# The fourth pair's bit rows: from SyncE's DMA queue to GpSimd's own queue

## The chip, the cores and the metric

The kernel runs on one core of one Trainium2 chip. The metric is device time in microseconds (us), lower is better; times are medians of several executions. TensorE (PE) multiplies matrices, VectorE (DVE), ScalarE (ACT) and GpSimd (POOL) work elementwise, and SyncE (SP) issues nearly all DMAs. Each engine carries out its own instructions in order and waits for others through semaphores; a DMA is issued by an instruction in one engine's order and lands later.

## The reference

Hash attention, then a gated feed-forward block with a residual. For 4 batches, 8 heads, 768 positions and 64 dimensions per head, a query sees only the keys that fall into its own hash bucket; the bucket is given by the signs of 6 projections.

```python
q_bits = (np.einsum('bhsd,dk->bhsk', q, proj) > 0)
k_bits = (np.einsum('bhsd,dk->bhsk', k, proj) > 0)
mask = q_bucket[:, :, :, None] == k_bucket[:, :, None, :]
scores = np.where(mask, scale * (q @ k.T), -1e9)
attn = softmax(scores)                      # over the keys
x = (attn @ v)                              # heads side by side: 3072 x 512
g, val = x @ w_gate, x @ w_val              # 512 -> 1536
ffn = (gelu(g) * val) @ w_out               # 1536 -> 512
out = x + sigmoid(x @ w_res) * ffn
```

## The kernel before

The 32 heads are worked on as 16 pairs, numbered 0 to 15; the fourth pair is number 3, the sixth number 5. Four pairs make a batch. For a pair, q and k (tiles `ld`) and v (`ldv`) are loaded. q and k are cast to bf16 (`cast`, tile `nat`) and transposed, mostly by a DMA transpose on SP (`transpose_dma`, into `aug`). `aug` holds the first head's 64 transposed dimensions; those of the second head are copied by GpSimd into the lower half of a tile `second` (`move_second`, L214).

The mask is put into the matmul itself. VectorE transposes blocks of q and k (`blocks`, L245, tile `t`), TensorE multiplies them with the projections (`hash_half`, L282), VectorE makes the signs (`hb`, L288) and shuffles them into the right partitions (`spread`, L297, tile `bits`). Then `mask_rows` (L322 to L329) moves seven rows of signs for each head and side into `aug` or `second` by four small DMAs, 10.5 KB each, two to `second` and then two to `aug`. With these rows the score matmul gives a large bonus to keys of the same bucket, and the exponential does the rest. So scores of a pair (L441, tile `sp`) can't start before its rows have landed.

A pair's scores are made in 9 chunks (12 for pair 0). For a chunk TensorE makes scores into one of two `sp` banks, ScalarE takes the exponential (L445, `e`), and two chunks later TensorE multiplies it with the values (L412) into the one `av` bank. At the pair's end VectorE normalises (`rec` L388, `x_tok` L389), which frees that bank, and TensorE transposes the outcome into `x_sb`. At a batch's end gate and value matmuls (`gate_val`, L463) follow, four chunks into the next batch, and the projection (`project`, L483 and L498) is spread over the chunks of the next batch.

The order is written by hand: `at(slot, f, ...)` puts work into a chunk's slot, and each engine gets its instructions in the order in which slots and tasks are walked through. `b1`, `b2` and `b3` are the first slots of pairs 1, 2 and 3. Within a slot the order of the `at` calls decides. No planner changes it on this path. Pools decide what has to wait: three `ld` buffers per side, two of `ldv`, `nat` and `bits`, four of `aug`. SP takes its DMAs one after the other; one of them waiting for a buffer or an earlier DMA holds the rest.

Around the change, in pair 1's last slots, SP issues loads of pair 3's v and of q and k of pairs 6 and 7, then pair 3's rows, then pair 4's v, its transposes and the first weight loads (`load_w`, L179). GpSimd has `move_second` of pair 3, the casts of pair 5, then `values_prep` of pair 3 (v to bf16 and sums over v, L332 to L340), then `move_second` of pair 4. Pair 1's rows are already divided between the two queues: `at(7, mask_rows, 1, (nc.sync, nc.gpsimd))`.

Of the kernel before, what the change touches and what calls it, by code (L numbers as in the profile page):

```python
# [17 lines left out]
def kernel(  # L18
# [12 lines left out]
    nc = tc.nc  # L31
# [485 lines left out]
    def base(p):  # L517
        return order.index((p, 0))
# [10 lines left out]
    def at(slot, f, *args):  # L529
        if f in (hash_half, transpose_pe):  # L530
            uses_tp.add(slot)
        tasks[slot].append(lambda: f(*args))
        busy[slot] += cost.get(f, 0.0)
# [88 lines left out]
    b1, b2, b3 = (base(i) for i in (1, 2, 3))  # L622
# [25 lines left out]
        at(b1 + 7, spread, 3, a)  # L648
    for side in range(2):
        at(b1 + 6, move_second, (3, side))  # L650
        at(b1 + 7, cast, (5, side))
        at(b1 + 7 + side, blocks, (5, side))
    at(b1 + 7, load, 7, (0, 1))
    at(b1 + 8, mask_rows, 3)
    at(b1 + 8, values_prep, 3)

    at(b2, load, 4, (2,))
# [139 lines left out]
```

## Time and profile before

| | |
|---|---|
| median of 6 runs | 348.25 us (347.44 to 349.45) |
| the profiled execution | 348.09 us, of which its span from the first to the last instruction 346.3 us |
| TensorE busy | 333.6 us, 96% of the span |
| ScalarE busy | 210.6 us, 61% |
| VectorE busy | 153.2 us, 44% |
| GpSimd busy | 153.2 us, 44% |
| DMA | 44.04 MB, mean 127 GB/s |
| exponentials, L445 | 147 of them, 143.7 us, mean 1007 ns |
| TensorE clock granted | 0.999 |

The share of busy time is a mean over stages. Up to about 53 us the first batch's attention runs without other work for TensorE beside it; afterwards feed-forward matmuls fill it. In a timeline each line has the start, the duration, the engine, the source line, the operation and its tiles; brackets hold the idle time before it and what ended it. SPq is SP's queue of DMA issues: the duration there is that of issuing, not of the transfer.

### The profile page before, as it was taken

The page shows a single profiled execution, that of the slowest core. Times are in us where ns is not written, and L with a number is a line of the kernel's source. Part 1 is how long each engine was busy: PE and PEld are TensorE (multiplying, and loading weights), DVE is VectorE, ACT ScalarE, POOL GpSimd, SP SyncE. Part 2 cuts the span into 40 slices and gives each one's busy share as a digit, 9 for nine tenths or more (in the row PEclk, how much of TensorE's full clock was granted, in tenths as well). Part 3 has the DMA queues.
Part 4 walks back from the last instruction along what each step waited for, and adds up shares of the span by engine and source line. Part 5 has one row for each costly group of instructions (what it writes and reads, how often), then busy time and mean ns, then how long its engine had stood idle before and what let it go on. Part 6 is the DMA issues. An engine that isn't in the chain of part 4 may idle for free.

```text
span 346.3 us, 7432 instructions
## 1 busy us (share of the span) xinstructions
PE 333.6 (96%) x2961; PEld 196.2 (57%) x3010; DVE 153.2 (44%) x280; ACT 210.6 (61%) x238; POOL 153.2 (44%) x198
## 2 busy tenths in 40 slices
PE   8889789999999999999999999999999999999995
PEld 4555556565565565655456566565556665665443
DVE  7986822333136526333444446343452026334243
ACT  6889885325898885223888788223788883332220
POOL 5899486864479585200068589300038222000000
PEclk9999999999999999999999999999999999999999
DMA  7977999997706964720014783600003321000012
GB/s 223 273 239 197 284 337 195 328 345 148 257 8 171 213 200 80 212 92 2 0 38 129 196 190 105 163 5 1 2 3 93 55 55 61 2 0 2 30 61 91
DMA packets 52717, 44.04 MB, mean 127 GB/s; under 512 B 31656, under 2 KB 44620, under 8 KB 52684
## 3 DMA queue, kind: packets, MB, share of 16 engines
q1 hardware_dynamic: 52540, 43.56, 45.3%
q8 instruction: 23, 0.38, 0.4%
q14 instruction: 10, 0.08, 0.1%
q0 software_dynamic: 64, 0.02, 0.0%
q10 hardware_dynamic: 80, 0.00, 0.0%
HBM read 29.36 MB, written 6.29 MB: 103 GB/s over the span
## 4 chain that ended last, share of the span: by engine, by line
PE 83%; ACT 4%; DVE 4%; POOL 3%; DMA 2%; issue 2%; SPq 1%; DVEq 0%; ACTq 0%; POOLq 0%
PE sp L463 36%; PE fps L498 16%; PE sp L441 13%; PE av L412 8%; PE rps L483 5%; ACT e L445 4%; PE hs L282 4%; DMA ld<-in_k_dram 2%; SPq L95 1%; DVE x_tok L389 1%; POOL ldv L338 1%; PE tp L398 1%; POOL o L507 1%; DVE o L504 1%; DVE total L382 1%
## 5 line engine op out<-in xcount | busy, mean ns | idle before, releaser
L445 ACT ACTIVATE e<-sp 128x1024 bf16<-128x1024 f32 (+1 forms) x147 | 143.7, 1007 | 25.4 <-PE sp L441 22.1
L469 ACT ACTIVATE gt<-sp 128x768 bf16<-128x768 f32 x48 | 38.9, 811 | 83.0 <-PE sp L463 83.0
L470 DVE SCALAR_TENSOR_TENSOR hh<-gt,sp 128x768 bf16<-128x768 bf16 x48 | 45.8, 954 | 81.4 <-PE sp L463 81.4
L498 PE MATMUL fps<-wo,hh 128*128 128x512 bf16 (+2 forms) x285 | 74.3, 369 | 1.3
L463 PE MATMUL sp<-x_sb,wg 128*128 128x256 bf16 (+1 forms) x376 | 70.3, 325 | 0.4
L463 PE MATMUL sp<-x_sb,wv 128*128 128x256 bf16 (+1 forms) x376 | 69.8, 325 | 0.6 <-DVE hh L470 0.2
L412 PEld LDWEIGHTS <-e 128*128 128x128 bf16 x1152 | 50.3, 97 | 33.5 <-issue 8.7
L441 PE MATMUL sp<-aug,aug 71*128 71x512 bf16 x192 | 54.3, 326 | 3.0 <-ACT e L445 2.9
L412 PE MATMUL av<-va,e 128*128 128x65 bf16 x1152 | 56.1, 193 | 1.0 <-DVE x_tok L389 0.3
L463 PEld LDWEIGHTS <-wv 128*128 128x128 bf16 x384 | 37.5, 98 | 25.2 <-issue 0.4
L463 PEld LDWEIGHTS <-wg 128*128 128x128 bf16 x384 | 37.2, 98 | 24.4
L441 PE MATMUL sp<-second,second 128*128 128x256 bf16 (+1 forms) x174 | 47.4, 320 | 0.3 <-ACT e L445 0.3
L507 POOL TENSOR_TENSOR o<-o,x_tok 128x512 f32<-128x512 f32 x18 | 20.8, 1156 | 56.7 <-DVE o L504 49.4
L498 PEld LDWEIGHTS <-hh 128*128 128x128 bf16 x300 | 28.6, 97 | 27.1
L504 DVE SCALAR_TENSOR_TENSOR o<-th,fps 128x512 f32<-128x512 f32 (+2 forms) x25 | 16.5, 661 | 52.7 <-PE fps L498 41.4
L389 POOL TENSOR_TENSOR x_tok<-total,rec 128x768 bf16<-128x768 f32 x9 | 13.3, 1472 | 45.0 <-DVE rec L388 45.0
L214 POOL COPY second<-aug 64x768 bf16<-64x768 bf16 x29 | 23.6, 825 | 19.6 <-DMA aug<-nat 12.9
L245 DVE STREAM_TRANSPOSE t<-ld 128x768 f32<-128x768 f32 (+1 forms) x34 | 29.5, 903 | 3.9 <-DMA ld<-in_q_dram 3.5
L486 ACT ACTIVATE th<-rps 128x512 f32<-128x512 f32 x24 | 14.3, 596 | 18.7 <-PE rps L483 14.3
L483 PE MATMUL rps<-wr,x_sb 128*128 128x512 bf16 x96 | 24.6, 379 | 0.0
L441 PEld LDWEIGHTS <-second 128*128 128x128 bf16 x192 | 18.5, 98 | 5.6 <-issue 2.5
L441 PEld LDWEIGHTS <-aug 71*128 71x128 bf16 x192 | 16.2, 97 | 6.7 <-issue 1.7
(71 smaller groups left out, 231.0 us busy)
## 6 DMA issues: line engine op xcount, KB each, us to landing
ldv<-in_v_dram SPq DMA_DIRECT2D x16, 384.0 KB
out_dram<-o SPq DMA_DIRECT2D x23, 256.0 KB
ld<-in_q_dram SPq DMA_DIRECT2D x15, 384.0 KB
ld<-in_k_dram SPq DMA_DIRECT2D x15, 384.0 KB
ws<-in_moe_w_gate_dram SPq DMA_DIRECT2D x6, 512.0 KB
ws<-in_moe_w_val_dram SPq DMA_DIRECT2D x6, 512.0 KB
ws<-in_moe_w_out_dram SPq DMA_DIRECT2D x6, 512.0 KB
ws<-in_moe_w_res_dram SPq DMA_DIRECT2D x2, 512.0 KB
```

What stands on the lines that cost most here:

```text
L214: eng.tensor_copy(second[x[0] % NM][x[1]][D:P], aug[x][D:P])
L245: nc.vector.transpose(t32[x][:, c0:c1].rearrange("p c h n -> p (c h n)"), raw[x][:, c0:c1].rearrange("p c d -> p (c d)"))
L412: nc.tensor.matmul(o[:, qt0 + i, :], e[:, off + i * P:off + (i + 1) * P], va[:, hi, jt, 0:D + 1], start=(hi not in begun), stop=(jt == T - ...
L441: nc.tensor.matmul(sp[:, off:off + nq * P], ks[0:n, jt, :], qs[0:n, qt0:qt0 + nq, :], start=True, stop=True)
L445: nc.scalar.activation(e[:, 0:n], sp[:, 0:n], AF.Exp, scale=float(ALPHA))
L463: nc.tensor.matmul(sp[:, c0:c1], w[:, kk, bass.ts(m, P)], xs[:, kk, c0:c1], start=(kk == 0), stop=(kk == KM - 1))
L469: nc.scalar.activation(gt, sp[:, 0:S], AF.Gelu)
L470: nc.vector.scalar_tensor_tensor(hh[:, m, :], gt, 0.5, ps[1][:, 0:S], op0=ALU.mult, op1=ALU.mult)
L483: nc.tensor.matmul(rps, x_sb[b][:, kk, t, :], wr[:, kk, :], start=(kk == 0), stop=(kk == KM - 1))
L498: nc.tensor.matmul(fps, hh[:, m, bass.ts(t, P)], wo[:, m, cs], start=(m == 0), stop=(m == KF - 1))
L504: nc.vector.scalar_tensor_tensor(o[:, cs], th[:, cs], 1.0, fps, op0=ALU.add, op1=ALU.mult)
L507: last.tensor_add(o3, o3, x_tok[b][:, k0:k1, t, :])
```

## The change

`mask_rows` of pair 3 goes from slot `b1 + 8` to slot `b1 + 7`, and its four DMAs are issued by GpSimd instead of SP. The two casts of pair 5 go from slot `b1 + 7` to `b1 + 8`, so that on GpSimd they follow these DMAs. On SP the four are gone from between the loads of pair 7 and the load of pair 4's v; the order of everything else on every engine is unchanged.

```diff
     for side in range(2):
         at(b1 + 6, move_second, (3, side))
-        at(b1 + 7, cast, (5, side))
         at(b1 + 7 + side, blocks, (5, side))
+
+    at(b1 + 7, mask_rows, 3, (nc.gpsimd, nc.gpsimd))
+    for side in range(2):
+        at(b1 + 8, cast, (5, side))
     at(b1 + 7, load, 7, (0, 1))
-    at(b1 + 8, mask_rows, 3)
     at(b1 + 8, values_prep, 3)
```

## The prediction

> **What bounds the kernel now.** I read the page first (TensorE busy 96% of a span of 346.3 us), then the list of waits, then the timelines of each queue and engine around the rows that move. The rows are those of pair 3, the fourth. Their wait stands in the list of waits between 24 and 60 us:
>
> ```profile
> PEld L441 <- DMA aug<-bits: 1.2, 1, 1.2
> ```
>
> It happens once. The timelines of the weight loads, of TensorE and of ScalarE place it (columns: start, duration, engine, line, operation, tiles; in brackets the idle time before and its releaser):
>
> ```profile
> 39.46 0.10 PEld L441 LDWEIGHTS <-aug 71*128 71x128 bf16 x1 [1.24 <-DMA aug<-bits]
> 39.49 0.38 PE L441 MATMUL sp<-aug,aug 71*128 71x512 bf16 x1 [1.15 <-ACT e L445]
> ...
> 35.41 3.87 ACT L445 ACTIVATE e<-sp 128x1024 bf16<-128x1024 f32 x4 [0.23 <-PE sp L441]
> 40.18 4.69 ACT L445 ACTIVATE e<-sp 128x1024 bf16<-128x1024 f32 x5 [0.90 <-PE sp L441]
> ```
>
> The first scores of pair 3 (L441) stand still until the rows land at about 39.4; the releaser beside the matmul is only inferred, the weight load in front of it shows the DMA. In this stretch the exponentials pace the work, one per 0.92 us. ScalarE's last four before the gap end at 39.28, the next starts at 40.18: 0.90 us are lost. Why the rows are late, from SP's queue:
>
> ```profile
> 31.27 0.41 SPq L95 DMA_DIRECT2D ld<-in_k_dram  x1
> 31.77 1.60 SPq L329 DMA_DIRECT2D second<-bits  x2
> 33.48 1.48 SPq L329 DMA_DIRECT2D aug<-bits  x2
> 35.22 0.39 SPq L95 DMA_DIRECT2D ldv<-in_v_dram  x1
> ```
>
> They stand behind five loads of 384 KB issued from 29.04 on. The last of the four is issued at about 34.2 (half of the 1.48 us after 33.48) and lands 5.2 us later; from 31 to 38 the DMA engines are busy 0.96, 327 GB/s.
>
> GpSimd's queue shows the gap into which the rows go, and what POOL asks for two such DMAs (for pair 1, earlier):
>
> ```profile
> 16.72 0.74 POOL L329 DMA_DIRECT2D second<-bits  x1
> 17.46 0.52 POOL L329 DMA_DIRECT2D aug<-bits  x1
> ...
> 29.97 1.59 POOL L214 COPY second<-aug 64x768 bf16<-64x768 bf16 x2
> 31.65 0.83 POOL L200 TENSOR_SCALAR nat<-ld 128x768 bf16<-128x768 f32 x1
> ...
> 41.05 1.59 POOL L214 COPY second<-aug 64x768 bf16<-64x768 bf16 x2 [4.88 <-PE av L412]
> ```
>
> What is late next is on VectorE, and in the scores after it:
>
> ```profile
> 35.23 0.98 DVE L245 STREAM_TRANSPOSE t<-ld 128x768 f32<-128x768 f32 x1 [3.15 <-DMA ld<-in_q_dram]
> ...
> 38.99 1.83 DVE L245 STREAM_TRANSPOSE t<-ld 128x768 f32<-128x768 f32 x2
> 41.05 0.23 DVE L388 RECIPROCAL rec<-av 128x12 f32<-128x12 f32 x1 [0.23 <-PE av L412]
> 41.31 0.96 DVE L389 TENSOR_TENSOR x_tok<-av,rec 128x768 bf16<-128x768 f32 x1
> ...
> 42.61 0.65 PE L412 MATMUL av<-va,e 128*128 128x65 bf16 x16
> 43.09 0.38 PE L441 MATMUL sp<-aug,aug 71*128 71x512 bf16 x1
> ```
>
> VectorE works without a pause from 35.23, when the load of pair 6's q lands, to 40.82. Only then can it normalise pair 2 (rec, x_tok), which frees the one av bank for pair 3's 16 value products. In this kernel it waits only 0.23 us there for TensorE.
>
> **What the Trainium skill says.** "DMA: Bandwidth & Descriptors", Queues, rings and completion order: each DMA engine takes turns between its queues, packet by packet. So rows on another queue need not wait out the loads. No DMA from POOL meets a full load in this trace (0.71 busy from 16 to 20 us); the nearest is ScalarE's small proj load, issued at 0.73 beside four loads and waited for until 3.59, 2.9 us. Same page, Anatomy of one DMA: about 2.0 us fixed for a DMA from GpSimd; the trace has 1.8 and 1.9 us from issue to landing. Same page, Issuing engines are not separate DMA queues: another issuer saves only the sequencer's time. For SP that is 3.1 us of issue here. "GPSIMD Engine Reference", Specifications: GpSimd shares its SBUF interfaces with VectorE, so more POOL work beside VectorE's run could stretch it. The trace shows no such stretch: a 128x384 shuffle takes 0.55 us at 38 us with POOL idle and 0.55 at 120.5 beside a POOL multiply.
>
> **The change, part by part.**
> Four DMAs onto POOL. Their data, the shuffles of pair 3, end at 29.14, and the copies in front of them on POOL end at 31.56, so nothing new is waited for. Issue: 0.74 + 3 x 0.52 = 2.3 us, from 31.6 to 33.9, the last started at 33.4. It lands at 33.4 + 1.8 = 35.2, or at 36.3 with the 2.9 us of the loaded case. These are the two bounds if the queues take turns. If they don't, the old 5.2 us give 38.6. I take 35.2 to 36.3.
>
> The first scores of pair 3. TensorE's last products before the wait start at 37.94 and leave it free at about 38.2; the score bank is free when the exponential before last ends, about 38.3. So the scores start near 38.3 instead of 39.49, and ScalarE goes on at 39.2: a gain of 0.9 to 1.0 us at this place. The rows have 2 us of slack, or lose it in the no-turns case (38.6: gain 0.8).
>
> What then holds. The scores of pair 3's fourth chunk would move from 42.17 to 41.2 and the 16 value products from 42.61 to 41.65. But VectorE ends its run at 40.82 whatever TensorE does, since it starts from a load that the change does not move. rec at 40.85 and x_tok (its start 0.26 later, 0.96 long) end at 42.07, not at 41.3. The products start at 42.1: 0.5 us earlier than before, not 0.95. The next scores come after them in TensorE's order: 43.09 becomes 42.6, done at 43.2, while ScalarE has been free since 42.85. From here on TensorE leads again (the hash matmuls at 43.62 follow directly; VectorE's transpose for them ends at 42.95 instead of 43.16), so 0.5 us is what goes on. The rows' 28 packets now overtake loads. At 4 x 7 x 1.5 KB = 43 KB against 327 GB/s that is 0.13 us at most for pair 6's loads, and so for VectorE's run. I take off 0.05. Gain: 0.45 us.
>
> Casts of pair 5 on POOL: 31.65 becomes 34.0, 2.3 us later. Their reader is a transpose on SP at 50.13. Behind them pair 3's values end at 38.5 instead of 36.18; TensorE first reads them at 42.1, the sums at 47.9. Both are hidden; 3.5 us are left for the first. Then POOL idles until 41.05 for pair 4's transposes: 4.88 us of cover. Without it the 2.3 us would delay the weight casts from 45.63 on, which have 3 us before TensorE's first gate matmul at 53.1.
>
> SP without the four: pair 4's v load, its transposes and four weight loads are issued up to 3.4 us earlier. Nothing on TensorE waits for them here. They fill the hole of 39 to 40 us (DMA busy 0.19), so pair 4's rows, issued 41.62 to 44.7 and needed at 49.07 (then 48.6), come no later. Cost and gain nothing.
>
> After 53 us the gate matmuls, the projection and the next batch follow in TensorE's fixed order, so what is won is kept: 0.45 us. The profiled run: 348.09 - 0.45 = 347.64, span 345.85; its 1.79 us outside the span stay. It lies 0.16 us below the median of the six runs, so the median becomes 348.25 - 0.45 = 347.8 us.
>
> **The rivals.** *The whole stall is won.* If VectorE's run ends earlier, say because pair 6's q lands sooner, 0.9 to 1.0 us carry on: 347.3. For it: the gap on ScalarE. Against it: that load is issued at 29.68, before anything the change touches. Chance 0.2.
> *Nothing is won.* The rows share the loads' backlog, or VectorE's run is pushed back by the rows' packets and POOL's adds beside it by as much as was gained: 348.25. Chance 0.13.
> *Slower: the rows land late on the software queue.* Each DMA from POOL could take much longer under full load than the 1.8 us seen at a lighter one. It decides from a landing at 39.4, 5.9 us after the last issue. At 41.0 the first scores lose 1.6 us, and that is on the path: 349.8. For it: no trace of such a DMA in this traffic. Against it: the small load beside full traffic took 2.9 us. Chance 0.17, which also holds what I can't see.
> The case worked out above has 0.5.
>
> **How the numbers follow.** About 0.3%, 1.04 us, is what a measurement of this kernel can tell from no change. My case alone spans 347.4 to 348.2. The range to 8 in 10 reaches down to 347.1, so that the whole-stall case lies in it, and up to 349.1, half of the slow case. Faster by over 0.3% (below 347.2): nearly half of the whole-stall case and a little of mine, 0.12. Slower (above 349.3): most of the slow case, 0.16. Same: 0.72.
>
> **What would show it.** Right: in the list of waits no wait of L441 for aug<-bits near 38 us; ScalarE's gap of 0.90 gone; POOL's four DMAs from 31.6 to 34; VectorE's rec directly behind its transposes at 40.85, and TensorE waiting there up to 0.5 us for x_tok; gate matmuls (L463) starting at 52.65 instead of 53.12. Wrong: pair 6's q landing away from 35.2, x_tok moving by more than 0.3 us, rows landing after 38.3, or the gain at 53 us not found again at the end.

## The result and the profile after

The changed kernel takes 349.3 us (median of 35 runs) against 348.4 us for the kernel before beside it (72 runs): a ratio of 1.0029, interval 1.0015 to 1.0044. A second measurement of it gave 1.0037 (1.0017 to 1.0056). So it is about 1 us slower, just at the edge of what can be told from no change, where 347.8 us and a small gain had been forecast. Its profiled execution took 349.48 us, with a span of 347.7 us against 346.3.

The wait that the change was to remove is still there, and longer. The list of waits between 24 and 60 us of the changed kernel:

```profile
PEld L441 <- DMA aug<-bits: 1.6, 1, 1.6
```

It was 1.2 us before. The timelines of the weight loads, of TensorE and of ScalarE around it (start, duration, engine, line, operation and tiles; in brackets the idle time before and its releaser):

```profile
40.62 0.10 PEld L441 LDWEIGHTS <-aug 71*128 71x128 bf16 x1 [1.64 <-DMA aug<-bits]
40.65 0.38 PE L441 MATMUL sp<-aug,aug 71*128 71x512 bf16 x1 [1.54 <-DMA aug<-bits]
...
36.17 3.87 ACT L445 ACTIVATE e<-sp 128x1024 bf16<-128x1024 f32 x4 [0.25 <-PE sp L441]
41.34 4.69 ACT L445 ACTIVATE e<-sp 128x1024 bf16<-128x1024 f32 x5 [1.30 <-PE sp L441]
```

ScalarE's gap in front of pair 3's first exponential has grown from 0.90 to 1.30 us. The queues of GpSimd and SP in the changed kernel:

```profile
31.34 0.83 POOL L214 COPY second<-aug 64x768 bf16<-64x768 bf16 x1 [0.43 <-DMA aug<-nat]
32.12 1.11 POOL L329 DMA_DIRECT2D second<-bits  x2
33.22 1.03 POOL L329 DMA_DIRECT2D aug<-bits  x2
34.32 0.82 POOL L200 TENSOR_SCALAR nat<-ld 128x768 bf16<-128x768 f32 x1
...
41.21 1.59 POOL L214 COPY second<-aug 64x768 bf16<-64x768 bf16 x2 [2.37 <-DMA aug<-nat]
```

```profile
32.02 0.41 SPq L95 DMA_DIRECT2D ld<-in_k_dram  x1
32.48 0.46 SPq L95 DMA_DIRECT2D ldv<-in_v_dram  x1
33.05 5.79 SPq L209 DMA_TRANSPOSE aug<-nat  x2
38.88 1.09 SPq L179 DMA_DIRECT2D ws<-in_moe_w_gate_dram  x2
```

GpSimd issues the four DMAs in 2.13 us, the last of them half a microsecond before SP's old last issue though this trace runs 0.76 us late, and has 2.37 us of idle time left in front of pair 4's copies. What is new is on SP: the load of pair 4's v goes out at 32.48 (before: 35.22) and the first of pair 4's two transposes at 33.05 (before: 36.23). They now stand beside the rows. The trace also records when each DMA raises its completion semaphore; read from there (us from the span's start):

| | before: issued, landed | after: issued, landed |
|---|---|---|
| load of pair 7's q | 30.76, 37.34 | 31.51, 38.39 |
| load of pair 7's k | 31.27, 38.45 | 32.02, 39.29 |
| the four rows of pair 3 | last at 34.26; last landed 39.40 | 32.12, 32.71, 33.22, 33.73; landed 38.59, 39.47, 40.37, **40.54** |
| load of pair 4's v | 35.22, 40.18 | 32.48, 40.47 |
| first transpose of pair 4 | 36.23, 40.91 | 33.05, 41.05 |

In both kernels the small rows land close to the place that their issue gives them among the 384 KB loads. On GpSimd's queue the first three come 0.1 to 1.0 us ahead of the load that was issued last before them, the fourth 0.07 us behind it; none comes past the loads issued earlier. A queue of their own didn't bring them past the backlog.

VectorE, where the prediction saw the next limit:

```profile
36.16 0.98 DVE L245 STREAM_TRANSPOSE t<-ld 128x768 f32<-128x768 f32 x1 [3.32 <-DMA ld<-in_q_dram]
...
39.92 1.82 DVE L245 STREAM_TRANSPOSE t<-ld 128x768 f32<-128x768 f32 x2
42.20 0.23 DVE L388 RECIPROCAL rec<-av 128x12 f32<-128x12 f32 x1 [0.46 <-PE av L412]
42.47 0.96 DVE L389 TENSOR_TENSOR x_tok<-av,rec 128x768 bf16<-128x768 f32 x1
```

It is done with its transposes at 41.74 and then waits 0.46 us for TensorE (0.23 before): it is not what holds.

**Where the 1.40 us between the two spans arise.** All of the changed trace is already 0.76 us later at the end of pair 0 (rec at 22.27 against 21.51), which is before the change acts. In two other traces of the changed kernel that point lies at 20.97 and 21.45, in two of the kernel before at 22.02 and 21.88, so this part is chance. From there to the first gate product (`hh`, L470) 0.39 us are added; ScalarE's gap alone has grown by 0.40. From that product to the end come 0.25 us more, and they come in the last 3 us: VectorE's last addition is late by 1.13 us, the end by 1.40. The traces of the two kernels, three of each:

| | before (3 traces) | after (3 traces) |
|---|---|---|
| gap before pair 3's first exponential | 0.90, 0.30, 1.67; mean 0.96 | 1.30, 1.04, 2.17; mean 1.50 |
| rows landed, after pair 7's k | 0.95, 0.79, 0.83; mean 0.86 | 1.25, 1.20, 1.52; mean 1.32 |
| end of pair 0 to first `hh` | 34.98, 34.78, 35.74; mean 35.17 | 35.37, 35.13, 37.01; mean 35.84 |
| first `hh` to the end | 289.81 to 289.82 | 290.06 to 290.16 |

The gaps scatter as much as they differ, since the loads ahead land at other times in each execution. The rows' distance from the load ahead of them and the end don't scatter so. The trace with 2.17 (x11) has a mean granted clock of 0.995; all of that is one stretch of 3.41 us from 41.3 on, in which TensorE was granted half its clock. It begins 0.6 us after the wait has ended, so it didn't cause this gap; it adds to the 37.01.

### The profile page after: what moved, and what is told of

It reads as the page before. It is cut to its first block, busy times and chain, and to the rows that moved or that the text cites. A ratio compares the mean times of both kernels' runs of the same rounds, so it can differ in the third digit from the quotient of the medians.

```text
span 347.7 us, 7432 instructions
## 1 busy us (share of the span) xinstructions
PE 335.0 (96%) x2961; PEld 197.0 (57%) x3010; DVE 153.2 (44%) x280; ACT 210.6 (61%) x238; POOL 155.3 (45%) x202
## 4 chain that ended last, share of the span: by engine, by line
PE 78%; POOL 7%; DMA 5%; DVE 4%; issue 2%; SPq 1%; ACT 1%; POOLq 0%; DVEq 0%; ACTq 0%
PE sp L463 35%; PE fps L498 16%; PE sp L441 11%; PE av L412 8%; PE rps L483 5%; PE hs L282 2%; DMA ld<-in_k_dram 2%; DMA aug<-bits 2%; POOL ldv L338 1%; ACT e L445 1%; SPq L95 1%; DVE x_tok L389 1%; POOL va L332 1%; POOL second L214 1%; DMA aug<-nat 1%
## 5 line engine op out<-in xcount | busy, mean ns | idle before, releaser
L470 DVE SCALAR_TENSOR_TENSOR hh<-gt,sp 128x768 bf16<-128x768 bf16 x48 | 45.8, 954 | 81.4 <-PE sp L463 81.4
L441 PE MATMUL sp<-aug,aug 71*128 71x512 bf16 x192 | 54.3, 326 | 3.5 <-ACT e L445 1.7
L441 PE MATMUL sp<-second,second 128*128 128x256 bf16 (+1 forms) x174 | 47.4, 320 | 0.2
L441 PEld LDWEIGHTS <-second 128*128 128x128 bf16 x192 | 18.6, 98 | 5.0 <-issue 1.9
L441 PEld LDWEIGHTS <-aug 71*128 71x128 bf16 x192 | 16.2, 97 | 7.2 <-issue 1.7
```

Source lines behind the costliest of these rows:

```text
L441: nc.tensor.matmul(sp[:, off:off + nq * P], ks[0:n, jt, :], qs[0:n, qt0:qt0 + nq, :], start=True, stop=True)
L470: nc.vector.scalar_tensor_tensor(hh[:, m, :], gt, 0.5, ps[1][:, 0:S], op0=ALU.mult, op1=ALU.mult)
```

## The experiments

Two theories stood against each other after the result. *Order*: the rows are late because taking them from SP lets pair 4's v and transposes move up beside them. *Software queue*: a DMA from GpSimd is itself slow under load. A third was that GpSimd's delayed casts cost something. Diffs are against the kernel before unless they say otherwise; ratios are to the kernel before beside the run.

**The changed kernel and the kernel before, again.** No edit. x1 and x5 were timed; x11 and x12 ran once each, for the spread of the traces.

> The changed kernel once more, unaltered, for a second trace and a paired time. In the first trace all of the run was already 0.75 us later at 21.5 us, before the change has any effect, and 0.40 us more came in at the first scores of pair 3, where the rows landed 6.8 us after their issue on POOL. If the loss is the late rows: the stall at these scores is again over 1.15 us (1.3 to 2), with the rows landing 6 to 7.5 us after issue, and the time is 0.3 to 1.0 us above the kernel before. If the loss was a slow start drawn by chance: the stall is 1.15 us or less, and the time equals that of before.

> The kernel before, unaltered, for a second trace and for what a comparison of a kernel with itself shows: ratio 1.000, within 0.002. For the stall at pair 3's first scores: if the first trace is typical, 0.7 to 1.2 us and rows landing 4.5 to 5.5 us after their last issue; if that trace had drawn a slow DMA engine, less than 0.5 us, and then the changed kernel's loss against it is larger than the 0.15 to 0.40 us that its two traces show against the one of before.

> The changed kernel, a third trace. Rows land 1.0 to 1.4 us after the last load of pair 7 (1.25 and 1.20 in the first two), beside or behind pair 4's v load. From pair 0's rec to the first gate product 35.1 to 35.7 us (35.37 and 35.13).

> The kernel before, a third trace. Rows land 0.7 to 1.0 us after the last load of pair 7 (0.95 and 0.79), and before pair 4's v load has landed. From pair 0's rec to the first gate product 34.6 to 35.1 us (34.98 and 34.78), 0.2 to 0.6 us less than the changed kernel.

Changed kernel: 349.61 us, 1.0037 (1.0017 to 1.0056). Kernel before: 348.67 us, 0.9991 (0.997 to 1.0013). The single executions took 350.31 us (changed) and 349.2 us (before); both missed what was forecast for the stretch to the first `hh`, by 1.3 and 0.6 us. The wait for the rows, from the weight loads' timeline of x1 and then of x5:

```profile
39.08 0.10 PEld L441 LDWEIGHTS <-aug 71*128 71x128 bf16 x1 [1.39 <-DMA aug<-bits]
```

```profile
39.77 0.10 PEld L441 LDWEIGHTS <-aug 71*128 71x128 bf16 x1 [0.63 <-DMA aug<-bits]
```

In x11 it was 2.52 us, in x12 2.00. The loss is repeatable over many runs; one pair of traces alone would not carry it.

**Rows first on SP (x2).** No queue is changed, only the rows' place: ahead of pair 7's loads.

```diff
+    at(b1 + 7, mask_rows, 3)
     at(b1 + 7, load, 7, (0, 1))
-    at(b1 + 8, mask_rows, 3)
```

> Rows of pair 3 stay on SP, but in front of the loads of pair 7 instead of behind them; casts and POOL as before. Theory backlog (a row lands when what was queued on the DMA engines before it is done, whichever queue it is on): two loads less are ahead, about 2.3 us at 327 GB/s, so the rows land near 37 us instead of 39.4 and the stall of 1.15 us is gone; ScalarE's gap of 0.90 goes, VectorE then holds half of it back; time 0.3 to 0.7 us below the kernel before. Loads of pair 7 come about 3 us later; if that pushes VectorE's blocks of pair 7 (39 us and 42 us) the gain is eaten: 0 to plus 0.5. Theory that the rows are late for a reason of their own (one slow DMA engine): landing stays near 39, time as before.

348.48 us, ratio 1.001 (0.9992 to 1.0027): the forecast gain didn't come. The rows landed at 36.55, 2.75 us after the start of their last issue, and pair 3's wait was gone. ScalarE:

```profile
36.06 8.45 ACT L445 ACTIVATE e<-sp 128x1024 bf16<-128x1024 f32 x9 [0.24 <-PE sp L441]
...
50.19 2.86 ACT L445 ACTIVATE e<-sp 128x1024 bf16<-128x1024 f32 x3 [0.56 <-PE sp L441]
```

Nine exponentials run through the old gap, and on VectorE `rec` and `x_tok` stand directly behind the transposes, as the prediction had it:

```profile
38.94 1.83 DVE L245 STREAM_TRANSPOSE t<-ld 128x768 f32<-128x768 f32 x2
40.85 0.23 DVE L388 RECIPROCAL rec<-av 128x12 f32<-128x12 f32 x1
41.12 0.96 DVE L389 TENSOR_TENSOR x_tok<-av,rec 128x768 bf16<-128x768 f32 x1
```

That the run ends within 0.05 us of the old place is partly luck: pair 6's q landed at 34.23, 1.0 us sooner than before, and VectorE then waited 0.65 us for TensorE in front of L399. The run does depend on TensorE.

Nothing can be measured at the end. The wait stands one pair later, in the weight loads' timeline:

```profile
49.48 0.10 PEld L441 LDWEIGHTS <-aug 71*128 71x128 bf16 x1 [0.86 <-DMA aug<-bits]
```

Pair 4's rows landed at 49.44. In the kernel before they landed at 49.02 and TensorE came for them at 49.07: there was next to no slack; in x5 and x12 it even waited about 0.2 us there. So x2 loses here most of what it won at pair 3. In the changed kernel pair 4's rows land sooner, 26.87 us after the end of pair 0 against 27.51 before, so whether it would have lost as much is not shown.

**The changed kernel with the SP issues put back (x3, x8).** GpSimd issues the rows as in the changed kernel; SP, where they stood, issues four copies of the same rows into memory that isn't in use then. Both runs are the same edit, against the changed kernel:

```diff
     at(b1 + 7, load, 7, (0, 1))
+    at(b1 + 8, rows_again, 3)
     at(b1 + 8, values_prep, 3)
```

> The changed kernel, and SP additionally issues four DMAs of the same shape and source where the rows stood before, into an unused part of the weight tile (extra work, the output is the same). So SP sends pair 4's v load and transposes as late as in the kernel before. Theory transposes: the earlier transposes of pair 4 held the rows back; then the rows on POOL land by 36 to 37.5 us and the stall is gone, time 0.3 to 0.5 below before. Theory backlog, or that POOL's queue is slow by itself: the rows on POOL still land 5.5 to 7 us after issue, near 39 to 40, stall 1.0 to 1.8 us, time as the changed kernel.

> The changed kernel with four extra copies of the rows on SP, once more: its first trace was taken at a granted clock of 0.99 with one DMA engine 1.8 us behind. If the earlier v load and transposes of pair 4 cost the changed kernel its time: the rows land within 0.5 us after the last load of pair 7 (1.2 us after it in the changed kernel), and the time is 0.5 to 1.2 us below the changed kernel's, near that of before. If POOL's queue by itself: 1 us after it, time as the changed kernel.

348.68 us, 1.0014 (0.9988 to 1.004), and 348.77 us, 1.0002 (0.998 to 1.0024): the time is about that of the kernel before again, though the rows still come from GpSimd and its casts are still late. The intervals overlap with the changed kernel's, x3's for the greater part, so the trace has to say it more plainly. Of x8, the timelines of the weight loads, ScalarE and SP (the copies push this kernel's line numbers up by 6; "wo" is where they go):

```profile
40.12 0.10 PEld L447 LDWEIGHTS <-aug 71*128 71x128 bf16 x1 [1.14 <-DMA aug<-bits]
...
36.17 3.87 ACT L451 ACTIVATE e<-sp 128x1024 bf16<-128x1024 f32 x4 [0.25 <-PE sp L447]
40.83 1.94 ACT L451 ACTIVATE e<-sp 128x1024 bf16<-128x1024 f32 x2 [0.79 <-PE sp L447]
...
32.53 2.98 SPq L335 DMA_DIRECT2D wo<-bits  x4
35.90 0.39 SPq L95 DMA_DIRECT2D ldv<-in_v_dram  x1
```

This trace runs in step with that of the changed kernel until the gap (both have ScalarE's four exponentials at 36.17) and goes on 0.51 us sooner: 40.83 against 41.34. The rows landed at 40.08, only 0.31 us behind the load ahead of them, against 1.25. That is the clearest single reading for the order. x3's trace is poorer evidence: one DMA engine was behind the rest, so that pair 7's k landed only at 41.16, and TensorE waited 2.88 us; there too the rows came close (0.19 us) behind that load. (Its low mean clock of 0.99 comes from half clock after this wait, from 43.0 on.) Of x3's forecasts none came true as a whole: the rows landed late, and the time was about that of before.

**Pair 4's v ahead of the rows, all on SP (x9).** None of pair 3's rows is on GpSimd; against the kernel before only the v load moves up.

```diff
+    at(b1 + 8, load, 4, (2,))
     at(b1 + 8, mask_rows, 3)
...
-    at(b2, load, 4, (2,))
```

> The kernel before with one step on SP changed: pair 4's v load goes in front of pair 3's rows instead of behind them; nothing is on POOL. Theory position (DMAs land about in the order of their issue on whichever queue; on POOL the rows came behind pair 4's v load, which on SP had stood behind them): one load more, 0.393 MB at 327 GB/s, is ahead, so the rows land about 1.2 us later than before, near 40.6 us, and the time is 0.6 to 1.2 us above before, like the changed kernel. Theory POOL's queue: the landing depends on the queue and not on the place, so rows near 39.5, time as before.

349.91 us, ratio 1.0048 (1.0031 to 1.0065). The weight loads and SP's queue:

```profile
40.62 0.10 PEld L441 LDWEIGHTS <-aug 71*128 71x128 bf16 x1 [2.02 <-DMA second<-bits]
...
31.38 0.46 SPq L95 DMA_DIRECT2D ldv<-in_v_dram  x1
31.93 1.76 SPq L329 DMA_DIRECT2D second<-bits  x2
```

The rows landed 1.96 us behind pair 7's k instead of 0.86, with the v load at 39.82 between. The difference of 1.10 us is about what the load itself takes (384 KB at the 327 GB/s of the kernel before: 1.2 us). Without GpSimd's queue, one load in front makes a loss like the change's. Three cautions. In this trace TensorE has half its clock for 3.41 us from 41.4 on, behind the wait, and so in part of the timed executions; but the nine of 20 with a mean clock of 0.998 or more still have a median of 349.45 us, against 348.31 for the 24 of 25 such ones of the kernel before. The trace also has a stall of 0.7 us at 31 us, at hash matmuls (L282) that the edit doesn't touch, and I can't say how many of the timed runs share it. And here the whole load stands ahead, in the changed kernel it stands beside the rows; so the size of this loss isn't that of the change.

**Rows from GpSimd, behind the casts (x10).** GpSimd's casts stay where they were.

```diff
-    at(b1 + 8, mask_rows, 3)
+    at(b1 + 8, mask_rows, 3, (nc.gpsimd, nc.gpsimd))
```

> Pair 3's rows on POOL as in the changed kernel, but behind the two casts of pair 5 instead of ahead of them: issued 1.6 us later, from 33.3 to 35.6. Theory position: then both of pair 4's transposes are issued on SP before the last rows, so the rows land near the end of the transposes, 40.5 to 42 us, 0.3 to 1.0 us later than in the changed kernel, and the time is 0.3 to 1.0 us above the changed kernel's (350 or more). Theory POOL's queue with a delay of its own (6.7 us from issue to landing): 1.6 us later, 42.2, time 1.3 us above the changed kernel's. If the delayed casts of pair 5 were what cost time: faster than the changed kernel.

352.63 us, ratio 1.0114 (1.0085 to 1.0142). The weight loads and GpSimd:

```profile
42.48 0.10 PEld L441 LDWEIGHTS <-aug 71*128 71x128 bf16 x1 [3.83 <-DMA aug<-bits]
...
33.48 1.11 POOL L329 DMA_DIRECT2D second<-bits  x2
34.57 1.03 POOL L329 DMA_DIRECT2D aug<-bits  x2
```

Issued 1.35 us later than in the changed kernel, the rows land 1.9 us later, at 42.44, among pair 4's transposes (41.98 and 42.66). With the casts not delayed it is much slower, so the delayed casts are not the cost. Between the two theories this run doesn't decide: for a delay of GpSimd's queue a landing at 42.2 had been forecast, for the order 40.5 to 42. Nor are the 4.3 us by which it is slower the price of the late landing alone: all six executions had a mean clock of 0.99 to 0.995, and in the trace TensorE has half its clock for 3.41 us from 43.7 on, behind the wait.

**Pair 7's loads behind pair 4's transposes (x4).** Against the changed kernel. The rows have two loads fewer in front.

```diff
-    at(b1 + 7, load, 7, (0, 1))
...
+    at(b2, load, 7, (0, 1))
```

> The changed kernel with the loads of pair 7 (q and k) issued behind pair 4's transposes. Of five loads of 384 KB in front of the rows, three are left. Theory backlog: the rows on POOL land 2 to 2.5 us sooner, 4 to 5 us after issue, at 36 to 37.5 us, no stall at pair 3's first scores. Theory POOL's queue slow by itself: 6 to 7 us after issue as in the changed kernel, stall over 1 us. Theory transposes (now even earlier against the rows): 6 to 7 us too. The time: VectorE's blocks of pair 7 may come later, so no clear statement, 0.5 us below before to 1 us above.

349.52 us, ratio 1.0037 (1.0019 to 1.0055): no better than the changed kernel. TensorE and SP:

```profile
39.70 0.39 PE L441 MATMUL sp<-aug,aug 71*128 71x512 bf16 x1 [1.62 <-DMA aug<-bits]
...
30.47 0.41 SPq L95 DMA_DIRECT2D ldv<-in_v_dram  x1
31.05 4.44 SPq L209 DMA_TRANSPOSE aug<-nat  x2
```

The rows landed at 39.65, 6.9 us after their last issue, in the company of what had moved up: v at 37.13, the transposes at 39.07 and 39.88. Taking backlog away from the front helped nothing, as SP's queue at once moved other work into its place. The 6.9 us are what had been forecast both for a slow GpSimd queue and for transposes in the way; this run doesn't tell the two apart. That the transposes weigh more than their bytes is suggested by it, not shown.

**Rows from ScalarE's queue (x7).**

```diff
-    at(b1 + 8, mask_rows, 3)
+    at(b1 + 7, mask_rows, 3, (nc.scalar, nc.scalar))
```

> Pair 3's four rows issued by ScalarE, a third queue, at the same place in the schedule as POOL has them in the changed kernel; POOL and SP otherwise as there. ScalarE loses about 4 x 0.56 us for the issues, on the path, so the time says nothing (plus 1 to 2.5 us); what is read is when the rows land. If POOL's queue is the cause (it completes only when all 16 DMA engines have passed the rows): on ScalarE's queue 7 engines count, and the rows land 0.5 to 1.5 us sooner against the last load of pair 7 than in the changed kernel, where they landed 1.2 us after it. If the freed SP stream (pair 4's v and transposes beside the rows) is the cause: again 1 us or more after it.

One execution, 352.55 us. ScalarE's queue and engine:

```profile
31.56 1.54 ACTq L329 DMA_DIRECT2D aug<-bits  x2
33.20 1.94 ACT L445 ACTIVATE e<-sp 128x1024 bf16<-128x1024 f32 x2 [3.62 <-POOL nat L200]
```

ScalarE lost 3.6 us to the issues and to the wait in front of the later ones, so the time says nothing of the rows. Their landing does: issued up to 32.4, the last landed at 36.89, 4.5 us later, just ahead of pair 7's q (issued 31.61, landed 37.17). On this third queue, too, a small DMA keeps about its place among the loads. By the reading that was set down for this run, rows well ahead of pair 7's k, it would count for GpSimd's queue as the cause. But SP issued that k only at 33.20 here, after the rows, so their coming 1.66 us before it doesn't decide.

**Both pairs' rows first (x6).** x2 moved the wait to pair 4, so here pair 4's rows also go ahead, of two weight loads and of pair 5's v.

```diff
+    at(b1 + 7, mask_rows, 3)
     at(b1 + 7, load, 7, (0, 1))
-    at(b1 + 8, mask_rows, 3)
...
-    for i in range(NWS):
+    for i in range(2):
         at(b2 + 1, load_w)
     at(b2 + 3, values_prep, 4)
-    at(b2 + 6, load, 5, (2,))
...
+    at(b2 + 8, mask_rows, 4)
+    for i in range(2):
+        at(b2 + 8, load_w)
+    at(b2 + 8, load, 5, (2,))
...
-    at(b3, mask_rows, 4)
...
-        at(b2 + 5 + i, cast_w)
+        at(b2 + 5 + i if i < 2 else b2 + 8, cast_w)
```

> Pair 3's rows on SP in front of pair 7's loads, and pair 4's rows in front of the last two of the four weight loads (and of pair 5's v load), whose casts follow one to three slots later on POOL. In the trace with pair 3's rows first, pair 4's rows landed at the very moment when TensorE wanted them and took half of the gain back. If these two waits are all: pair 4's rows land about 3 us sooner, no wait of L441 for them, the gate matmuls start 0.5 to 0.9 us sooner than in the kernel before against pair 0's end, and the time is 0.4 to 0.9 us below before. If the weight loads held back become the next wait: gate matmuls wait for weight casts, time as before or 1 us above.

**347.42 us, ratio 0.9963 (0.9943 to 0.9983)**: faster than both kernels. ScalarE:

```profile
36.01 8.45 ACT L445 ACTIVATE e<-sp 128x1024 bf16<-128x1024 f32 x9 [0.23 <-PE sp L441]
44.95 2.04 ACT L445 ACTIVATE e<-sp 128x1024 bf16<-128x1024 f32 x2 [0.49 <-PE sp L441]
47.53 4.99 ACT L445 ACTIVATE e<-sp 128x1024 bf16<-128x1024 f32 x5 [0.54 <-PE sp L441]
```

Pair 4's rows landed at 45.93, well before TensorE comes for them, and no L441 waits for a DMA here any more. What is left between the exponentials are gaps of about 0.5 us behind TensorE's hash matmuls. From the end of pair 0 to the first `hh` it takes 33.96 us, against a mean of 35.17 before.

## Why the prediction was wrong

Two steps failed: one took the gain away, the other made the loss.

**"SP without the four ... Cost and gain nothing" is the step behind the loss.** It did see that pair 4's v and transposes would be issued up to 3.4 us earlier (measured: 2.7 and 3.2, in a trace that runs 0.76 us late). It asked who on TensorE waits for these, and for what would stand in the hole at 39 us, and not beside what they would now land. They came into the same stretch as the rows, which had stood in front of them. x8 puts the four issues back, and with them the time; x9 moves the v load ahead on SP alone and gets a loss without GpSimd.

**The rows' landing, 35.2 to 36.3, and 38.6 at worst, is the step that took the gain.** Measured 40.54, 39.04 and 40.64 in the three traces. The bounds came from DMAs at light load (1.8 us) and from a small load among the first four (2.9 us). With the DMA engines busy 0.97 between 31 and 38 us, the last row took 6.6 to 7.7 us in the three traces. The Trainium skill ("DMA: Bandwidth & Descriptors", Queues, rings and completion order) says that an engine takes turns between its queues, packet by packet, from which I concluded that the rows need not wait out the loads. The landing times here don't bear that conclusion out, on GpSimd's queue or on ScalarE's. The third bound, "the old 5.2 us", took the time from issue to landing for a constant. The trace of before says otherwise: four rows issued over 2.5 us landed within 0.56 us (38.84 to 39.40), just behind pair 7's k. x8 takes SP's part out, and the rows from GpSimd's queue then land 17.8 us after the end of pair 0, where they landed 17.9 us after it from SP in the shown trace of before. The queue alone brings nothing. The same page's Issuing engines are not separate DMA queues says that DMAs interleave on the same engines whoever issued them; the trace agrees, with rows and loads landing among each other from 38.39 to 41.05.

**The slower rival had the mechanism in part.** It set its point at a landing of 39.4, and 349.8 us for 41.0. Measured: 40.54 in a trace that began 0.76 us late, and 349.3 us. But it named the software queue as the cause; x8, in which the rows come from GpSimd and nothing is lost, speaks for the order. One part of the queue's own may remain: on GpSimd's queue each row's semaphore was raised in 16 late steps, over 1.5 to 2.1 us, on SP's in seven. The same page, in Why a DMA increments its semaphore by 16 and not by 1, says that all 16 engines post an increment for a DMA from GpSimd, and only those that it uses for one from SP; the traces agree. With it, a row on GpSimd's queue waits for the slowest of 16 engines. How much it adds isn't separated; x8's 0.31 us leaves little room for it.

**Pair 4's rows "come no later".** True: 49.14, in a trace that runs 0.76 us late, and needed only at 50.2. But the prediction gave when those rows are issued and when they are needed, and didn't look up when they land: 49.02 before, for a need at 49.07. With that landing, the forecast need of 48.6 would have been missed by 0.4 us, nearly all of the forecast gain; the 0.6 us by which they came sooner in the changed kernel would have made up for it, but the prediction had not worked this out. x2 has pair 3's wait gone and `rec` at 40.85, but not SP's stream relieved. It measured 348.48 us, no gain (at best 0.08% by its interval), although its one trace is 0.5 us shorter than the shown one of before up to the first `hh`; that difference stays unexplained.

**What held.** GpSimd's issue, 2.3 us forecast, took 2.13. The delayed casts are hidden: 2.37 of the 4.88 us of cover were left, and x8 keeps them late at no cost. After 53 us what is lost is kept: the shift of 1.15 us at the first `hh` was 1.13 us at VectorE's last addition, 287 us later. Three signs under "Wrong" appeared: rows landing after 38.3, pair 6's q away from 35.2 (36.14) and `x_tok` moved by more than 0.3 us (42.47). The late start makes up most of the last two.

**The sum.** By the means of three traces the gap costs 0.54 us, and the end, below, 0.27: 0.8 us together. The two comparisons gave 1.0 and 1.3 us, with intervals from 0.5 to 2.0. Part of what is over goes with the granted clock. In the comparison of x1, six of 22 executions of the changed kernel had a mean clock below 0.998, and two of 59 of the kernel before; without these the medians are 349.05 and 348.11 us, 0.9 us apart. How often such executions come also differs from one comparison to the next (11 of 45 of the kernel before beside x5 to x8), so the exact share isn't settled. In x3 and x8 the stretch from the first `hh` to the end was 0.3 us shorter than before, which I can't explain either.

## What to carry to other kernels

Where the DMA engines were full in this kernel, the place in the order of issue decided when a small DMA landed, to within about 1 us, and not the queue that it was issued on. There it is worth trying to move it ahead of the large loads that nobody waits for yet, as x6 does. When a DMA is taken off a queue, list what stood behind it there, and ask whether that now competes with it. Before a wait is counted as won, look up the margin of the next wait of the same kind: here it was 0.05 us, and of x2 and x6 only x6, which removed both waits, gained.

## What the runs showed of the hardware that was not expected

*The end of the program depends on how many DMAs were issued elsewhere than from GpSimd.* From the start of VectorE's last addition to the end of the span it took 2.85 to 2.88 us in every trace of a kernel that issues as many DMAs from SP and ScalarE together as before (the kernel before three times, x2, x3, x6, x7, x8, x9), and 3.12 to 3.13 us in every one where four of them go to GpSimd (the changed kernel three times, x4, x10). The last operations, before and then after:

```profile
343.45 0.29 DVE L507 TENSOR_TENSOR o<-o,x_tok 128x128 f32<-128x128 f32 x1
343.77 0.33 SPq L510 DMA_DIRECT2D out_dram<-o  x1
```

```profile
344.58 0.29 DVE L507 TENSOR_TENSOR o<-o,x_tok 128x128 f32<-128x128 f32 x1
344.90 0.33 SPq L510 DMA_DIRECT2D out_dram<-o  x1
```

From the addition to the last store's issue both take 0.32 us. After it SP looks at the DMA semaphores in a fixed order, some 0.06 us apart. Before, the last store's semaphore is in the sixth of seven checks; after, the semaphores have been dealt out four places differently, the store's is in the fourth of nine, and the five checks behind it, which could have been done while the store was under way, come after it. This reading of the 0.27 us is from the events in the traces; no run changed it by itself.

*Small DMAs nearly keep their place across queues.* Rows of 10.5 KB for pair 1 took 1.7 to 2.9 us from issue to landing on GpSimd's queue (14 traces; DMA engines busy 0.71 from 16 to 20 us in that of before). Where the engines were full, pair 3's rows took 5.6 to 7.9 us on GpSimd's queue (three traces of the changed kernel), 5.1 to 7.1 us on SP's (the shown trace of before), and the last one 4.5 us on ScalarE's (x7), each within about 1 us of the loads issued just before.

*A wait of TensorE of about 2 us was followed by half its clock.* Between its first and its last matmul each of the 14 traces has at most one idle time of TensorE over 0.9 us, beside these rows or, in x7, beside ScalarE's issues. Where it was 1.91 us or less (nine traces) the clock stayed at full until TensorE's last matmul. Where it was 1.93 to 3.81 us (x9, x11, x3, x10, x7) TensorE was granted half its clock for 3.41 us, in x3 for 6.83, from 2.7 to 4.9 us after the idle time began. One such stretch takes 0.5% off an execution's mean clock, which is then 0.995. So the longer waits cost more than their own length, by an estimated 0.8 us in x11 against the shown trace of the changed kernel: 1.64 us longer from the end of pair 0 to the first `hh`, of which 0.87 are ScalarE's gap. No run set the length of the wait on purpose, so where the border lies is known no better than this.
